# Rows of x by products of 64x32 tiles in the last three batches, with a new planner rule and a new table

## The chip, the core and the metric

The kernel runs on one core of a Trainium2 chip. The core has a matrix engine (TensorE, "PE" in the profile, its weight loads "PEld"), three engines for element-wise work (VectorE "DVE", ScalarE "ACT", GpSimd "POOL") and queues that start DMAs (here nearly all from "SP"). TensorE reads SBUF and writes PSUM; VectorE and ScalarE copy from PSUM to SBUF. The metric is the device time of one execution in microseconds. The median of three runs before the change is 265.24 us (264.93 to 265.75).

## What is computed

The reference is an attention of the Nystrom kind over eight batches, eight heads, 576 tokens of 64 elements, followed by a layer with a norm, two weight matrices and a residual:

```
q_lm, k_lm = means of q, k over 32 segments of 18 tokens
A = softmax(q k_lm'), Bm = softmax(q_lm k_lm'), C = softmax(q_lm k')
Z = Bm' / (norms);  six times: Z = 2 Z - Z Bm Z
x = A Z C v                       per head, then laid out as (batch, 576, 512)
out = x + relu(norm(x) * g @ w1) @ w2      w1 512 x 2048, w2 2048 x 512
```

The change concerns how `x` is formed in the last three batches. For a batch, `x` is 576 rows of 512 columns. Each head gives 64 of the columns: the head's 32 columns of A (one for each landmark) times a 32 x 64 matrix, Z C v. `x` is needed for the statistics of the norm and for the residual; the first layer does not read it, because the kernel multiplies A by a product that it has already folded with w1.

## The kernel before, in words

**Tiles.** The rows of `x` of all batches lie in blocks of 128 (`x_blk`), 36 in all. A batch has 4.5 blocks: odd batches begin with half a block and even batches end with one. Four heads are handled as a unit `u` of 128 partitions, 32 landmarks each, so a batch has two units. For each unit `ea[u]` holds the scores of q (landmarks on partitions, tokens along the free axis), and `zcbd[u]` the matrix Z C v of its four heads, written block by block on the diagonal of a 128 x 256 tile; the rest of that tile is zero.

**Rows.** `rows_of` (line 808) forms one block at a time: two products of 128 x 128 weights (`ea`) and 256 columns (`zcbd`), one for each unit, into one bank of PSUM; then one copy of 512 columns to `x_blk`, on ScalarE or VectorE, whichever the planner expects to be done sooner (`sooner`). It is the last part of `attention2`, which forms the attention of one or two batches. `measure` then takes a block's statistics on VectorE, and `deviations` turns them into the factors of the norm that `finish_block` needs.

**First layer.** `First.two_products_of_heads` (line 1341) forms two of the four `m16` tiles of a batch: sixteen products of 64x32 tiles and 512 columns, eight of which run side by side, into two banks and one double bank, `psm`; four copies of 512 columns follow. It is called twice a batch. `chunk` then makes one of 16 row tiles of the hidden layer: four products of 288 columns into a double bank `psh`, and one copy with a relu to `hT`. All double banks are drawn from a pool of two (`ps2`, tag `p2`); the other four banks are handed out by `banks`.

**Second layer.** It multiplies `hT` by w2. From batch 4 on it uses seven products of halves in place of eight (`seven_products`), for which VectorE mixes parts of `hT` and GpSimd mixes parts of w2 ahead. The last 64 columns of an even batch's `hT` are copied by GpSimd into the next batch's (`keep_tail`).

**Order.** The kernel writes out one order of instructions for each engine. Five streams (attentions, totals, first layers, first rows, second layers) are generators; before each step a stream says when it could go, and `run` takes the first that can. The times come from a planner, class `Clock`: `note` books every instruction with an estimated duration (`took`) on its engine. Small work (loads, casts, turns, statistics, mixes) is put in between by `help_out`. The table `AFTER` holds exceptions found by search: an entry (k, n): (j, m) keeps the n-th step of kind k back until m steps of kind j are done. In `took`, an operation of VectorE of 1024 elements is given a longer time when GpSimd is busy; and after a centring of w1 the planner moves the time at which GpSimd is free.

**Buffers of zcbd.** There are four. A batch that is handled alone takes two of them by its parity, a pair of batches takes all four.

All VectorE, ScalarE and GpSimd instructions that the planner records have the helper's line 302 in the profile, and the matmuls line 308, so that groups are told apart by the names of tiles: `bank<-zcbd,ea` are the rows, `bank<-w,zt` and `psm<-w,zt` the products of heads, `psh<-ea,m` the chunks, `bank<-w,hT` and `bank<-w2mix` the second layer.

Of the kernel before, what the change touches and what calls it, by code (L numbers as in the profile page):

```python
# [10 lines left out]
FP32 = mybir.dt.float32  # L11
# [5 lines left out]
P = 128  # L17
# [3 lines left out]
def kernel(  # L21
# [63 lines left out]
    class Clock:  # L85
# [5 lines left out]
        def __init__(self):  # L91
            self.free = dict.fromkeys(("PE", "DVE", "Activation", "Pool", "SP"), 0.0)
            self.wrote, self.used, self.begun = {}, {}, {}
            self.small, self.lanes, self.wire = False, {}, 0.0
            self.cells, self.count, self.mark, self.fetched, self.ahead = [], 0, 95, 0.0, 0.0
            self.loads, self.pool = [], []
            self.free['PE'], self.issued = 1500.0, 0
# [33 lines left out]
        def took(self, i, e, n, m):  # L131
# [25 lines left out]
        def note(self, i):  # L157
# [70 lines left out]
            else:  # L228
                start = max(self.free[e], ready)
                self.ready = start  # L230
# [4 lines left out]
                if e == 'DVE' and count[0] == 1024 and writes[0] in parted_w1:  # L235
                    self.free['Pool'] = max(self.free['Pool'], start) + 430
# [573 lines left out]

    def rows_of(bs, ea, zcbd):
# [288 lines left out]
    def attention2(bs, c):  # L1100
# [113 lines left out]
        cv, z0 = cv_[0], 2 * (bs[0] % 2) if W == 2 else 0  # L1214
        yield lambda: clock.both(clock.at(st, cv), asm.next("zt"))
# [38 lines left out]
        yield from rows_of(bs, ea, zcbd_buf[z0:z0 + W])  # L1254
# [9 lines left out]
    def block_done(j):  # L1264
        unmeasured.append(j)

    def measure():
        j = unmeasured.pop(0)
        b, u = group_of(j)
        if u == 0:  # L1270
# [4 lines left out]
        blocks_done[b] = u + 1  # L1275
# [55 lines left out]
    class First:  # L1331
# [60 lines left out]
    def first_layer(b):  # L1392
# [5 lines left out]
        if two:  # L1398
            yield lambda: max(banks.next(2), ps2.next("p2"), mprod.next("m16", 2), clock.at(l1.zt))
            l1.two_products_of_heads(0)  # L1400
        else:
            yield lambda: max(banks.next(2), mprod.next("m16"), clock.at(l1.zt))
            l1.product_of_heads(0)
        for m in range(MCH):
            yield lambda: max(ps2.next("p2"), clock.at(l1.m16[m // 4], *l1.ea))
            l1.chunk(m)
            chunks[b] = m + 1
# [5 lines left out]
            if two and m == 4:  # L1413
                yield lambda: max(banks.next(2), ps2.next("p2"), mprod.next("m16", 2))
                l1.two_products_of_heads(2)
# [5 lines left out]
    chunks = {}  # L1421
# [242 lines left out]
    def help_out(hurry=False):  # L1664
# [226 lines left out]
```

## Time and profile before

| | |
|---|---|
| median of the runs | 265.24 us |
| the profiled execution, its own time | 265.93 us |
| its span, first to last instruction | 264.2 us |
| TensorE busy | 253.6 us, 3351 matmuls |
| VectorE busy | 209.4 us |
| ScalarE busy | 173.2 us |
| GpSimd busy | 136.0 us |
| rows of x, products | 80 of 128x256 |
| rows of x, copies of a whole block | 22 on ScalarE (596 ns), 10 on VectorE (688 ns) |

The profile is of one execution. Its page lists busy times by engine, a chain of the work that ended last, and groups of equal instructions with their mean duration and the idle time of the engine ahead of them. Matmuls are pipelined: their durations overlap, so what one occupies is read from the starts in the timeline. The timeline gives the start, the duration and, in brackets, how long the engine had stood idle and what ended that.

### The profile page before, as it was taken

What the parts mean: (1) busy time and instruction counts of PE and PEld (TensorE: products, weight loads), DVE (VectorE), ACT (ScalarE), POOL (GpSimd) and SP (SyncE); (2) the same over time, 40 slices, a digit from 0 to 9 for tenths busy, and PEclk for the clock granted to TensorE, in tenths of its full rate; (3) what the DMA queues carried; (4) which work ended last, traced back from release to release, by engine and by line L of the source; (5) the groups of instructions that cost most, each with busy time, mean ns of one, the idle gap of its engine ahead of it and who ended that gap; (6) DMA issues with size and microseconds to landing.
All of it is one profiled execution on the core that took longest, in us unless ns stands there. A gap on an engine that the chain in (4) does not pass through costs nothing.

```text
span 264.2 us, 8212 instructions
## 1 busy us (share of the span) xinstructions
PE 253.6 (96%) x3351; PEld 167.7 (63%) x3351; DVE 209.4 (79%) x466; ACT 173.2 (66%) x333; POOL 136.0 (51%) x162
## 2 busy tenths in 40 slices
PE   7899989999999999999999999999999999999994
PEld 6645754546456574546655466577877875788883
DVE  2677865999979987999998974999696868976762
ACT  2588886548686987588788687667666755873000
POOL 5288779999861889797799956600000005000000
PEclk9999999999999999999999999999999999999999
DMA  7999999999867896866951010110060006100605
GB/s 249 381 394 369 383 389 372 357 265 325 286 176 211 264 365 172 262 182 169 398 147 45 21 47 19 42 40 4 0 159 4 2 21 144 38 0 2 159 16 185
DMA packets 24125, 46.67 MB, mean 177 GB/s; under 512 B 2964, under 2 KB 3224, under 8 KB 24088
## 3 DMA queue, kind: packets, MB, share of 16 engines
q1 hardware_dynamic: 23608, 45.50, 54.0%
q10 hardware_dynamic: 480, 0.66, 0.8%
q8 instruction: 26, 0.43, 0.7%
q14 instruction: 11, 0.09, 0.1%
HBM read 36.70 MB, written 9.44 MB: 175 GB/s over the span
## 4 chain that ended last, share of the span: by engine, by line
PE 75%; DVE 11%; DMA 8%; ACT 2%; POOL 2%; issue 1%; SPq 0%; DVEq 0%
PE bank L308 49%; PE psh L308 20%; DMA stg<-in_k_dram 4%; DMA wstg<-in_moe_w_ch_dram 4%; DVE m L302 2%; DVE w L302 2%; PE pscv L308 2%; PE psd L308 2%; DVE xblk L302 1%; DVE six L302 1%; DVE part L302 1%; POOL w L302 1%; PE psea L308 1%; ACT lns L302 1%; DVE xT L302 1%
## 5 line engine op out<-in xcount | busy, mean ns | idle before, releaser
L308 PE MATMUL bank<-w,hT 128*128 128x512 f16 (+3 forms) x528 | 110.2, 335 | 0.0
L302 ACT ACTIVATE hT<-psh 128x576 f16<-128x576 f32 x119 | 74.3, 653 | 20.9 <-PE psh L308 19.2
L308 PEld LDWEIGHTS <-hT 128*128 128x128 f16 x656 | 60.8, 98 | 30.5 <-issue 5.7
L308 PE MATMUL psh<-ea,m 128*128 128x288 f16 x512 | 78.7, 286 | 0.1
L308 PEld LDWEIGHTS <-m 128*128 128x128 f16 x512 | 49.1, 98 | 19.1 <-issue 1.9
L302 DVE SCALAR_TENSOR_TENSOR xblk<-bank,rstd,xblk 128x256 f32<-128x256 f32 (+2 forms) x77 | 38.9, 540 | 12.6 <-PE bank L308 12.3
L302 POOL TENSOR_TENSOR ea<-ea,lns 128x576 f16<-128x576 f16 x14 | 17.9, 1286 | 52.0 <-ACT lns L302 51.6
L302 POOL CAST nat<-stg 128x1152 f16<-128x1152 f32 x23 | 26.9, 1186 | 12.9 <-DVE xT L302 7.1
L302 DVE BATCH_NORM_STATS2 six<-xblk 128x6 f32<-128x512 f32 x36 | 24.2, 673 | 1.7 <-ACT xblk L302 1.6
L302 POOL CAST natv<-stg 128x1152 f16<-128x1152 f32 (+1 forms) x17 | 19.3, 1163 | 11.0 <-DMA stg<-in_v_dram 7.8
L302 ACT COPY xblk<-bank 128x512 f32<-128x512 f32 (+1 forms) x29 | 16.6, 592 | 8.6 <-PE bank L308 8.4
L302 DVE STREAM_TRANSPOSE xT<-nat 128x576 uint32<-128x576 uint32 x28 | 21.3, 761 | 0.3 <-POOL nat L302 0.3
L302 DVE SCALAR_TENSOR_TENSOR st<-st,bank 128x128 f16<-128x128 f16 (+3 forms) x36 | 13.2, 366 | 9.2 <-PE bank L308 9.0
L308 PE MATMUL bank<-w2mix 128*128 128x256 f16 x128 | 17.9, 273 | 0.0
L308 PE MATMUL bank<-w2mix,hT 128*128 128x256 f16 x128 | 16.4, 272 | 0.0
L302 ACT ACTIVATE lns<-psd 128x576 f32<-128x576 f32 x16 | 10.3, 646 | 6.5 <-PE psd L308 6.3
L302 DVE TENSOR_REDUCE part<-xT 128x32 f16<-128x576 f16 x20 | 14.3, 740 | 0.1
L308 PE MATMUL bank<-zcbd,ea 128*128 128x256 f16 x80 | 14.3, 273 | 0.0
L308 PEld LDWEIGHTS <-st 32*32 32x32 f16 (+1 forms) x380 | 7.0, 90 | 11.4 <-DVE st L302 6.9
L308 PEld LDWEIGHTS <-w2mix 128*128 128x128 f16 x128 | 12.4, 98 | 2.5 <-issue 0.6
L302 POOL TENSOR_TENSOR asum<-asum 128x256 f32<-128x256 f32 (+1 forms) x20 | 12.8, 641 | 1.6
L302 ACT CAST m<-bank 128x512 f16<-128x512 f32 x16 | 9.2, 587 | 6.5 <-PE bank L308 6.3
(130 smaller groups left out, 372.2 us busy)
## 6 DMA issues: line engine op xcount, KB each, us to landing
stg<-in_q_dram SPq DMA_DIRECT2D x16, 576.0 KB, 6.4
stg<-in_k_dram SPq DMA_DIRECT2D x16, 576.0 KB, 6.1
out_dram<-xblk SPq DMA_DIRECT2D x66, 128.0 KB, 2.4
wstg<-in_moe_w_ch_dram SPq DMA_DIRECT2D x16, 512.0 KB, 7.6
stg<-in_v_dram SPq DMA_DIRECT2D x5, 576.0 KB, 8.5
stg<-in_v_dram SPq DMA_DIRECT2D x40, 72.0 KB, 3.0
stg<-in_v_dram SPq DMA_DIRECT2D x6, 288.0 KB, 5.1
stg<-in_v_dram SPq DMA_DIRECT2D x12, 144.0 KB, 4.0
```

The costliest lines, as they stand in the source:

```text
L302: return lambda *args, **kw: keep(getattr(self.engine, op)(*args, **kw))
L308: keep(nc.tensor.matmul(o, l, r, start=start, stop=stop, tile_position=(rb, cb), skip_group_check=(skip or cb != 0)))
```

## The change

It has three parts.

1. In batches 5 to 7 (`LATER = 5`) the rows of `x` are no longer formed by `attention2`. `rows_later` only notes which blocks there are and keeps `ea` and `zcbd`. `two_rows` forms two whole blocks at once, right behind `two_products_of_heads` (at both of its calls, `PAIRS = (0, 4)`), from 32 products of 64x32 tiles and 128 columns into one double bank `psr`; four copies of 256 elements for the two blocks, strided on the side of `x`, follow behind the copies of the products of heads. The contraction is over 64 partitions, that is two heads, and not 128. The half block of a batch is still formed by whole products (`part_of_rows`), behind chunk 8 of an even and chunk 6 of an odd batch. Four whole blocks in each of three batches make six groups.
2. In the planner, a centring of w1 no longer moves GpSimd's free time; it books an interval (`locks`), and a GpSimd operation that would begin inside of it begins at its end. An operation of 1024 elements on VectorE right behind such an interval is given 1600 ns in place of 1000 when GpSimd is busy for over 1000 ns more.
3. The table `AFTER` is new, with 67 entries (72 before), most of them different. The choice of `zcbd` buffers is new too: a batch alone takes the first two except batch 1, and an attention waits until rows that are still to be formed no longer need the buffers. `measure` counts blocks in place of taking the last one's number.

```diff
+    def crossed(x, hp):
+        n = 256 + 64 * (1 - 2 * hp)
+        v = x[:, 64 * hp:64 * hp + DM - 128]
+        return bass.AP(v.tensor, v.offset, [list(v.ap[0]), [n, 2], [2 * D, 2], [1, D]])
+
+    def two_rows(b):
+        ea, zcbd = row_zc[b]
+        mine = [row_blocks[b].pop(0) for _ in range(2)]
+        t = ps2.tile([P, 2, 512], FP32, name="psr", tag="p2")
+        to = t[:].rearrange("p h (i u c) -> p h i u c", i=2, u=U)
+        for i in range(2):
+            for u in range(U):
+                for c in range(4):
+                    for hp in range(2):
+                        MM(to[ds(32 * c, 32), hp, i, u, :],
+                           ea[u][ds(64 * hp, 64), ds(mine[i][1] + 32 * c, 32)],
+                           zcbd[u][ds(64 * hp, 64), :, :]
+                           .rearrange("p (r e) d -> p r e d", e=2)[:, :, hp ^ u, :],
+                           rb=64 * hp, cb=32 * c, skip=True)
+
+        def copies():
+            copy = sooner(1024, clock.at(t))
+            for i, (j, _) in enumerate(mine):
+                for hp in range(2):
+                    copy(crossed(x_of(j), hp), to[:, hp, i, :, :].rearrange("p u (r d) -> p u r d", r=2))
+                block_done(j)
+        return copies
...
             one = self.products(f, [banks.take([P, 512]), t[:, 0, :]])
             two = self.products(f + 1, [banks.take([P, 512]), t[:, 1, :]])
+            copies = two_rows(self.b) if 2 * f in PAIRS and self.b >= LATER else lambda: None
             self.copies(f, one)
             self.copies(f + 1, two)
+            copies()
...
-        cv, z0 = cv_[0], 2 * (bs[0] % 2) if W == 2 else 0
-        yield lambda: clock.both(clock.at(st, cv), asm.next("zt"))
+        cv, z0 = cv_[0], 2 * (bs == (1,))
+        mine_z = {name_of(t) for t in zcbd_buf[z0:z0 + W]}
+        yield lambda: (NEVER if any(name_of(t) in mine_z for _, z in row_zc.values() for t in z)
+                       else clock.both(clock.at(st, cv), asm.next("zt")))
...
-        yield from rows_of(bs, ea, zcbd_buf[z0:z0 + W])
+        yield from (rows_later if bs[0] >= LATER else rows_of)(bs, ea, zcbd_buf[z0:z0 + W])
...
             l1.chunk(m)
+            if m == PART[b % 2] and b in row_part:
+                part_of_rows(b)
...
                 last = max([b for a, b in self.pool if a <= self.ready < b] + [0.0])
-                queued = 1000 if self.free["Pool"] > self.ready else 690
+                next_ = self.locks and self.ready - self.locks[-1][1] < 150
+                queued = (690 if self.free["Pool"] <= self.ready else
+                          1600 if next_ and self.free["Pool"] > self.ready + 1000 else 1000)
...
+                if e == "Pool":
+                    for a, z in self.locks:
+                        if a <= start < z:
+                            start = z
...
                 if e == 'DVE' and count[0] == 1024 and writes[0] in parted_w1:
-                    self.free['Pool'] = max(self.free['Pool'], start) + 430
+                    self.locks = self.locks[-4:] + [(start, done)]
...
-    chunks = {}
+    chunks, PART, PAIRS, ONES = {}, (8, 6), (0,4), ()
+    LATER = 5
```

In the instructions: 24 products of 128x256 go and 192 of 64x32 tiles with 128 columns come, so that TensorE has 3519 matmuls in place of 3351. Twelve copies of whole blocks of rows become 24 copies of 256 elements, 16 on VectorE and 8 on ScalarE in the new order.

More of the change, by code (lines that the diff above doesn't have):

```diff
@@ L809, in iterate, with rows_later @@
         return stn
+    row_blocks, row_part, row_zc = {}, {}, {}
+    def rows_later(bs, ea, zcbd):
+        for i, b in enumerate(bs):
+            row_blocks[b] = []
+            row_zc[b] = ea[U * i:U * i + U], zcbd[U * i:U * i + U]
+            t0 = 0
+            while t0 < S:
+                j, pb = divmod(b * S + t0, P)
+                n = min(P - pb, S - t0)
+                if n == P:
+                    row_blocks[b].append((j, t0))
+                else:
+                    row_part[b] = j, pb, n, *((t0 + n - P, P - n) if pb == 0 else (0, 0))
+                t0 += n
+        for _ in range(5 * len(bs)):
+            yield lambda: 0.0
@@ new lines, in one_row, with part_ready, part_of_rows @@
+    def one_row(b):
+        ea, zcbd = row_zc[b]
+        j, at = row_blocks[b].pop(0)
+        xb = x_of(j)
+        psy = banks.take([P, 512])
+        for u in range(U):
+            MM(psy[:, ts(u, 4 * D)], ea[u][:, ds(at, P)], zcbd[u][:].rearrange("p h d -> p (h d)"))
+        sooner(512, clock.at(psy))(xb[:], psy)
+        block_done(j)
+    def part_ready(b):
+        return max(banks.next(2), 0.0 if row_part[b][0] in x_blk else xpool.next("xblk"))
+    def part_of_rows(b):
+        ea, zcbd = row_zc[b]
+        j, pb, n, at, side = row_part.pop(b)
+        xb = x_of(j)
+        psy = banks.take([P, 512])
+        for u in range(U):
+            MM(psy[:, ts(u, 4 * D)], ea[u][:, ds(at, P)], zcbd[u][:].rearrange("p h d -> p (h d)"))
+        sooner(512, clock.at(psy))(xb[ds(pb, n), :], psy[ds(side, n), :])
+        if pb + n == P:
+            block_done(j)
@@ L1404, in first_layer @@
         for m in range(MCH):
-            yield lambda: max(ps2.next("p2"), clock.at(l1.m16[m // 4], *l1.ea))
+            yield lambda: max(ps2.next("p2"), clock.at(l1.m16[m // 4], *l1.ea),
+                              part_ready(b) if m == PART[b % 2] and b in row_part else 0.0,
+                              max(banks.next(2), xpool.next("xblk")) if m in ONES and b >= LATER else 0.0)
             l1.chunk(m)
+            if m == PART[b % 2] and b in row_part:
+                part_of_rows(b)
+            if m in ONES and b >= LATER:
+                one_row(b)
+            if b in row_zc and not row_blocks[b] and b not in row_part:
+                row_zc.pop(b)
             chunks[b] = m + 1
```

14 lines of the change are left out of this document (10 added, 4 removed), and 33 rows, old and new, of the table AFTER.

## The prediction

> **What bounds the kernel now.** I read the page first (busy times, the chain of work that ended last), then the groups by form for the price of one instruction, then the timeline at the few places where TensorE stands still. The page says what kind of kernel this is:
>
> ```profile
> span 264.2 us, 8212 instructions
> PE 253.6 (96%) x3351; PEld 167.7 (63%) x3351; DVE 209.4 (79%) x466; ACT 173.2 (66%) x333; POOL 136.0 (51%) x162
> ...
> PE 75%; DVE 11%; DMA 8%; ACT 2%; POOL 2%; issue 1%; SPq 0%; DVEq 0%
> ```
>
> TensorE is busy 96% and holds 75% of the chain; from 72 us to the end the chain is almost TensorE alone. So a change pays by the matmul time that it removes, and by the places where TensorE waits. The granted clock is 1.00 in every stage, so columns turn into time at one rate. The prices, from the groups by form (last columns: busy us, mean ns of one, idle before):
>
> ```profile
> L308 PE MATMUL bank<-zcbd,ea 128*128 128x256 f16 x80 | 14.3, 273 | 0.0
> L308 PE MATMUL bank<-w,zt 64*32 64x512 f16 x144 | 10.9, 383 | 1.2 <-DVE xblk L302 0.9 <-ACT zt L302 0.3
> L302 ACT ACTIVATE ec<-psec 128x256 f16<-128x256 f32 x28 | 10.8, 474 | 0.9 <-PE psec L308 0.7
> L302 ACT COPY xblk<-bank 128x512 f32<-128x512 f32 x22 | 12.6, 596 | 3.9 <-PE bank L308 3.8
> L302 DVE COPY xblk<-bank 128x512 f32<-128x512 f32 x10 | 6.9, 688 | 1.6 <-PE bank L308 1.6
> L302 DVE TENSOR_TENSOR zcbd<-pszc,heads 128x256 f16<-128x256 f32 x14 | 5.0, 414 | 0.0
> L302 ACT CAST zt<-pszt 128x256 f16<-128x256 f32 x1 | 0.4, 353 | 0.0
> ```
>
> The mean of a pipelined matmul is latency; what it occupies is read from starts in the timeline (start us, us, engine, form):
>
> ```profile
> 74.00 0.72 PE L308 MATMUL pscv<-natv,ecT 64*64 64x130 f16 x36
> 74.66 0.42 PE L308 MATMUL psd<-ea,bones 128*128 128x288 f16 x2
> ...
> 82.55 0.38 PE L308 MATMUL bank<-zcbd,ea 128*128 128x256 f16 x2
> 82.77 0.38 PE L308 MATMUL bank<-w,hT 128*128 128x512 f16 x1
> ```
>
> Two whole products of 256 columns occupy 0.22 us, 0.11 each. Thirty-six products of 64x64 tiles and 130 columns, four at a time, are nine rounds: of the 0.66 us from 74.00 to 74.66 about 0.10 is the change of tile shape, which leaves 0.062 a round. By columns at the whole product's rate (0.11 for 256) a round would be 0.055.
>
> TensorE's largest wait after the start, in the timeline around the rows of batch 5:
>
> ```profile
> 169.21 2.15 DVE L302 TENSOR_TENSOR w2mix<-hT 128x1024 f16<-128x1024 f16 x2
> 169.78 1.04 POOL L302 COPY hT<-hT 128x1024 f16<-128x1024 f16 x1 [1.47 <-PE bank L308]
> ...
> 171.28 0.74 DVE L302 SCALAR_TENSOR_TENSOR xblk<-bank,rstd,xblk 128x512 f32<-128x512 f32 x1
> ...
> 172.07 0.37 PE L308 MATMUL bank<-w,zt 64*32 64x512 f16 x1 [0.93 <-DVE xblk L302]
> ```
>
> Two mixes on VectorE (0.68 each elsewhere) take 2.15 beside a copy on GpSimd, the update of x behind them starts late, its bank comes free at 172.02, and the second round of products of heads starts at 172.07 where 170.95 was possible: 1.1 us lost. Two smaller ones:
>
> ```profile
> 45.31 0.23 PE L308 MATMUL pszt<-st,cv 32*32 32x32 f16 x16
> 45.85 0.22 PE L308 MATMUL pszc<-cv,st 32*32 32x64 f16 x8 [0.31 <-ACT lns L302]
> ...
> 70.66 0.19 PE L308 MATMUL bank<-st,bones 128*128 128x64 f16 x1
> 71.40 0.29 PE L308 MATMUL bank<-st 128*128 128x128 f16 x2 [0.55 <-DVE st L302]
> ```
>
> About 0.4 us at 45 and, with 0.13 ahead of 70.66, 0.84 at 70.
>
> **The change part by part.** *The products.* Twelve blocks of rows (batches 5 to 7) lose 24 whole products: 24 x 0.110 = 2.63 us. They get 192 products of 64x32 tiles and 128 columns, eight tiles at a time, so 24 rounds in six groups of four. By columns a round is 0.055; at the spread of the 64x64 rows (0.062 for 130 columns) it is 0.061; the first round of that row, whose weights are loaded in the open, took about 0.08. The groups stand straight behind products of heads of the same 64x32 shape, and the order of the changed kernel has as many changes of tile shape as before (58), so none is added. I take 0.060, since weights for the first round can load during the 0.21 us of the round ahead: 24 x 0.060 = 1.44, **gain 1.2**; bounds 1.3 (0.055) and 0.7 (0.08). *The page's price:* "TensorE: Matmul & The Clock Gate" of the Trainium skill, Back-to-back issue gap, gives some 81 ns between matmuls of 128 columns in a stream of loads and matmuls; taken as the price of a round, the gain would be 0.7. No run here has that stream, and the 64x64 rows (0.062 a round) speak for less.
>
> *The copies.* Twelve copies of 512 become 24 of 256 strided elements, 16 on VectorE and 8 on ScalarE in the new order. VectorE: 16 x 0.42 = 6.7; ScalarE: 8 x 0.35 to 0.47 = 2.8 to 3.8. With the other copies shifted between them (whole-block copies 10 to 3 and 22 to 17, half blocks 1 to 4 and 7 to 4, first-layer outputs 9 to 6 and 119 to 122) VectorE gains about 1.7 us of work (6.7 - 4.8 + 2.1 - 2.3) and ScalarE stays within 1 us. Both have room as a total, so this costs only where TensorE waits for a copy.
>
> *The buffer.* A group's output takes the second of the two double-bank buffers that the chunks of the first layer rotate through. The second chunk behind a group therefore waits for its four copies, and the first for the copies of the products of heads. Hand-over costs 0.17 from TensorE (mean 286 for a 288-column matmul of 0.12) and 0.05 back (172.02 to 172.07). From the order: behind the first group of batch 7, TensorE has sixteen 256-column products and a change of shape (1.85 us) before the first chunk, and about 3.0 before the second. ScalarE alone carries four copies of products of heads (4 in 2.16 at 168.44, or 4 x 0.60), then four row copies (0.29 apart as the exps at 36.05, six in 1.74, or 0.47 each): the first chunk's buffer is free 1.9 to 2.2 after the group, the second's 3.1 to 4.0. I take 0.6 us of waiting here, 0.2 behind the first group of batch 5 (same four copies on ScalarE, rows on VectorE), 0.1 each behind the two of batch 6 (0.69 + 4 x 0.42 + 0.22 - 0.27 = 2.3 against 2.2 of cover), none behind the other two: **cost 1.0**, bounds 0 and 3.6 (below).
>
> *The wait at 172.* The rows of batch 5 no longer take banks before these products, and in the new order the last reader of either bank has 3 us or more of TensorE work between its input and the reuse. **Gain 1.1**; 0 if VectorE is as late again.
>
> *The new table.* It moves nearly everything after 32 us: loads, casts, turns, mixes. The SP queue issues the same DMAs with some stores and loads exchanged; DMA has room from 135 us on (share about 0.2). I looked at each wait above again. At 45 a pair of second-layer products now stands between, **gain 0.4** (0 to 0.5). At 70 VectorE has one centring of w and one statistics ahead of the softmax, not two centrings (0.98 mean each, 1.90 for the pair at 67.45): **gain 0.4** of 0.84 (0 to 0.84). At 35 the old wait of about 1.4 stays, in another form: a chunk now stands straight behind the scores and must wait for three exps. In batches 5 and 6 five chunks return to their buffer after 0.82 us of TensorE work, where the output's 0.653 and the 0.22 to 0.24 of hand-over need 0.89: **cost 0.35** (0 to 0.7).
>
> **The sum.** -1.2 + 1.0 - 1.1 - 0.4 - 0.4 + 0.35 = -1.75 us against the profiled execution: 265.93 to 264.2. That execution lies 0.69 above the median of 265.24, so the median goes to **263.5**.
>
> **The rivals.** *Evacuation turns into the bound (slower).* TensorE saves 0.2 us a group but every group now waits. This is a rule of "TensorEngine Tiling (Array Packing)" of the Trainium skill, Performance Considerations: tiles speed up TensorE and not the emptying of PSUM, which may become the bottleneck. In rows: if VectorE comes to the four groups that it copies about 0.6 later (at 171.28 it was over 1 us late beside GpSimd) and ScalarE's row copies cost 0.47 with its queue, the waits are 4 x 0.6 + 1.0 + 0.2 = 3.6 instead of 1.0: 263.5 + 2.6 = 266.1. It ends slower than before once the six groups wait over 2.75 in all, 0.46 each. For it: 79% busy VectorE. Against it: 1.85 to 4 us of cover in the order.
> *The waits only move.* The mixes and GpSimd's copies are the same instructions, and 2.15 for 1.36 of work shows what they do to a queue. If the new order has as much waiting as the old one where I see none, the gains of 1.1, 0.4 and 0.4 go: 263.5 + 1.9 = 265.4, or 264.5 if half of it comes true.
> *The tiles do not overlap.* If each round shows its weight load (89 ns for a 64x32 load, mean of the groups) before its 0.055, 24 x 0.145 = 3.5: 0.85 lost instead of 1.2 won, 263.5 + 2.05 = 265.5. The 64x64 rows speak against it.
>
> **How the numbers follow.** Forecast 0.52 (own range 262.4 to 264.4); evacuation 0.15; waits move 0.20, of which 0.05 stay under 264.4; no overlap 0.07; better than forecast (all waits gone, no new ones: 261.7) 0.06. A difference under 0.3% (0.8 us) is about what a measurement can't tell from none. Faster: 0.52 + 0.06 + 0.05 = 0.63. Within: 0.13 + 0.07 = 0.20. Slower: 0.15 + 0.02 = 0.17. The range reaches from 262.3 to 265.8: below it most of the 0.06, above it most of the evacuation.
>
> **What would show it.** Groups of four rounds that take 0.22 to 0.27 us; the two rounds of products of heads of batch 5 side by side; chunk tiles behind the groups with waits for copies of the row tile of 0.2 to 0.6 in batch 7; no wait of 0.5 us for a softmax in batch 2. Wrong would be: rounds above 0.08; waits for row copies of over 0.4 behind every group; a wait of over 1 us anywhere after 72 us.

## The result, and the profile after

The changed kernel takes 263.31 us in the median of eight runs (263.06 to 264.70). Beside them on the same chip the kernel before took 265.38 (eight runs, 264.93 to 265.75). The ratio is 0.9929 with a 95% interval of 0.9911 to 0.9947: 0.7% faster, 2.07 us.

The profiled execution of the changed kernel has an own time of 264.70 us, 1.4 above its median, where that of before lay 0.7 above. So its span is only 1.2 us shorter. The page:

```profile
span 263.0 us, 8556 instructions
PE 252.0 (96%) x3519; PEld 167.8 (64%) x3519; DVE 209.7 (80%) x475; ACT 171.5 (65%) x335; POOL 137.3 (52%) x163
...
PE 75%; DVE 10%; DMA 8%; ACT 3%; issue 1%; POOL 1%; SPq 0%; ACTq 0%; DVEq 0%
```

Nothing about the bound has changed: TensorE is busy 96% and holds 75% of the chain. It does 1.6 us less. The new groups, by form (busy us, mean ns of one, idle before):

```profile
L315 PE MATMUL bank<-zcbd,ea 128*128 128x256 f16 x56 | 9.9, 273 | 0.0
L315 PE MATMUL psr<-zcbd,ea 64*32 64x128 f16 x192 | 3.0, 217 | 0.0
L309 DVE COPY xblk<-psr 128x256 f32<-128x256 f32 x16 | 5.6, 414 | 0.0
L309 ACT COPY xblk<-psr 128x256 f32<-128x256 f32 x8 | 2.5, 432 | 0.0
L315 PE MATMUL psh<-ea,m 128*128 128x288 f16 x512 | 78.5, 286 | 1.0 <-ACT ec L309 0.9
```

Of the whole products of rows 56 are left. The copies cost what was predicted (0.42 and 0.35 to 0.47). The chunks (`psh`) stand idle for 1.0 us in all, and 0.9 of that is for exps at 35 us, not for row copies.

The place of the largest wait before, the products of heads of batch 5, in the timeline of after (start us, us, engine, form, idle before):

```profile
168.36 1.29 DVE L309 TENSOR_TENSOR w2mix<-w2mix,hT 128x1024 f16<-128x1024 f16 x2
169.32 1.23 POOL L309 COPY hT<-hT 128x1024 f16<-128x1024 f16 x1 [3.96 <-PE bank L315]
169.56 0.74 DVE L309 SCALAR_TENSOR_TENSOR xblk<-bank,rstd,xblk 128x512 f32<-128x512 f32 x1
...
169.67 0.39 PE L315 MATMUL bank<-w,zt 64*32 64x512 f16 x1
...
169.89 0.38 PE L315 MATMUL bank<-w,zt 64*32 64x512 f16 x1
...
170.11 0.48 PE L315 MATMUL psr<-zcbd,ea 64*32 64x128 f16 x32
...
170.53 1.92 PE L315 MATMUL bank<-w,hT 128*128 128x256 f16 x16
...
171.62 1.40 DVE L309 COPY xblk<-psr 128x256 f32<-128x256 f32 x4
```

The two rounds stand side by side (169.67, 169.89), where before 1.1 us lay between them. The two mixes ahead of the update of x take 1.29 us here, where before 2.15 stood, with GpSimd's copy of `hT` starting when they are nearly done; the update begins at 169.56 and not at 171.28. The second round does not even wait for it: the update ends at 170.30, the round starts at 169.89. By the semaphores in the trace (the signals by which one engine waits for another), its product into a bank waits for ScalarE, whose last signal came at 168.15; before, it waited for VectorE's at 172.03. The four rounds of rows begin at 170.11. From the first product of heads to the next whole product is 0.86 us (169.67 to 170.53). Products of heads without rows take 0.56 (46.41 to 46.97), so the rows cost 0.30 here; in batch 6 the same reading gives 0.88 (191.38 to 192.26), 0.32.

The two smaller places:

```profile
45.61 0.24 PE L315 MATMUL pszt<-st,cv 32*32 32x32 f16 x16
...
45.72 0.22 PE L315 MATMUL pszc<-cv,st 32*32 32x64 f16 x8
...
70.04 0.21 DVE L309 TENSOR_REDUCE rsum<-bank 128x2 f32<-128x64 f32 x1
...
70.36 1.15 POOL L309 TENSOR_TENSOR asum<-nat 128x512 f32<-128x512 f16 x1
...
70.77 0.19 PE L315 MATMUL bank<-st,bones 128*128 128x64 f16 x1 [0.60 <-DVE st L309]
71.03 0.76 DVE L309 TENSOR_TENSOR st<-bmT,mask 128x256 f16<-128x256 f16 x1
...
71.85 0.28 PE L315 MATMUL bank<-st 128*128 128x128 f16 x2 [0.89 <-DVE st L309]
```

The wait at 45 is gone. The one at 70 is not: TensorE stands still twice, 0.77 and 1.06 us counted from when the work ahead has run through, where before it was 0.13 and 0.72.

So the time is there, but not where I had put it. Theory A for the experiments: tiles and the place of the rows bring the gain. Its rival B: the new table does, and the tiles add nothing. Two smaller questions go with them: why a round costs 0.075 to 0.08 and not 0.06, and why the softmax of batch 2 got later.

### The profile page after: what moved, and what is told of

It is laid out like the page before. It is cut to its first block, busy times and chain, and to the rows that moved or that the text cites. A ratio compares the mean times of both kernels' runs of the same rounds, so it can differ in the third digit from the quotient of the medians.

```text
span 263.0 us, 8556 instructions
## 1 busy us (share of the span) xinstructions
PE 252.0 (96%) x3519; PEld 167.8 (64%) x3519; DVE 209.7 (80%) x475; ACT 171.5 (65%) x335; POOL 137.3 (52%) x163
## 4 chain that ended last, share of the span: by engine, by line
PE 75%; DVE 10%; DMA 8%; ACT 3%; issue 1%; POOL 1%; SPq 0%; ACTq 0%; DVEq 0%
PE bank L315 49%; PE psh L315 19%; DMA wstg<-in_moe_w_ch_dram 6%; DVE m L309 2%; DMA stg<-in_k_dram 2%; DVE w L309 2%; PE pscv L315 2%; PE psd L315 2%; ACT xblk L309 1%; DVE six L309 1%; PE psea L315 1%; DVE xblk L309 1%; DVE part L309 1%; ACT hT L309 1%; PE psec L315 1%
## 5 line engine op out<-in xcount | busy, mean ns | idle before, releaser
L309 ACT ACTIVATE hT<-psh 128x576 f16<-128x576 f32 x122 | 75.9, 653 | 22.5 <-PE psh L315 21.1
L309 POOL CAST nat<-stg 128x1152 f16<-128x1152 f32 x24 | 28.9, 1223 | 9.8 <-DMA stg<-in_v_dram 4.7
L315 PE MATMUL bank<-w2mix 128*128 128x256 f16 x128 | 17.3, 273 | 0.0
L309 ACT COPY xblk<-bank 128x512 f32<-128x512 f32 (+1 forms) x21 | 12.4, 594 | 5.9 <-PE bank L315 5.8
L309 ACT ACTIVATE ec<-psec 128x256 f16<-128x256 f32 (+1 forms) x42 | 11.9, 424 | 2.3 <-PE psec L315 2.0
```

What stands on the lines that cost most here:

```text
L309: return lambda *args, **kw: keep(getattr(self.engine, op)(*args, **kw))
L315: keep(nc.tensor.matmul(o, l, r, start=start, stop=stop, tile_position=(rb, cb), skip_group_check=(skip or cb != 0)))
```

## The experiments

**The changed kernel once more.** No edit.

> The changed kernel once more, unaltered, beside the kernel before on one chip. Both theories (the gain sits in the rows and the wait at 172; the gain sits in the new table) expect the same of it: 263.3 us, ratio to before 0.993. What it tells is how steady the places are: the wait of 1.34 us before bank<-nat,pairs at 25.9 (0.57 in the profile of before, where the instructions up to there are the same) should be back near 0.6 if it is an accident of one execution, and the two waits around the softmax of batch 2 (0.77 and 1.06 us, together 1.8 against 0.84 before) should stay at 1.8 if they belong to the new order, or fall to about 0.4 as predicted if they too are an accident.

263.56 us, ratio 0.9927 (0.9909 to 0.9945). The wait at 26 us was 0.78 in this execution. In the runs below, with the same program up to there, it was between none and 1.07: its length changes from one execution to the next, and 0.8 of the high time of the first profile is such an accident. The two waits of batch 2 stayed here, 0.78 and 1.05. But the next three runs have the same instructions up to the rows of batch 5, and there they are 0.89 and 0.71, 0.57 and 0.71, 0.48 and 0.72. So 0.4 to 0.8 us over the 0.84 of before belong to the order, and the rest to the execution; the last section shows what makes the second wait 1.05 or 0.71.

**Whole products in the same places.** The rows of the six groups by 24 whole products again. The planner still books the tiles, so that every engine keeps the order of the changed kernel; the copies now take adjacent columns (412 ns on VectorE and 432 on ScalarE; 414 and 432 with tiles).

```diff
-        for i in range(2):
-            for u in range(U):
-                for c in range(4):
-                    for hp in range(2):
-                        MM(to[ds(32 * c, 32), hp, i, u, :], ...)
+        for i in range(2):
+            for u in range(U):
+                MM(t[:, i, ds(256 * u, 256)], ea[u][:, ds(mine[i][1], P)],
+                   zcbd[u][:].rearrange("p h d -> p (h d)"), skip=True)
```

> The rows of the six groups are made by whole products again (four of 128x128 with 256 columns a group, copied out by four copies of 256), in the places and in the order of the changed kernel on every engine; only the tiles are undone. Theory A (the tiles pay what the trace of the change shows, 0.300 to 0.326 us a group, 1.88 in all, against 24 x 0.110 = 2.63 for whole products): 0.75 us slower than the changed kernel, so about 264.1, plus up to 0.1 us a group if the whole products make TensorE change its tile shape once more (about 0.10 at a change by the rows of 64x64 tiles at 74.0), which gives 264.1 to 264.7. The predicted price of 0.060 a round: 1.2 us slower, 264.5 (to 265.1). Theory B (the new table brings the gain, the tiles nothing): 263.3, no difference from the changed kernel.

264.18 us, ratio 0.995 (0.9934 to 0.9966): 0.62 above the run beside it. The two intervals overlap a little, but the traces agree with the size: a group of whole products takes 0.45 (168.92 to 169.37 in its timeline), of tiles 0.30 to 0.32, and from the last products of heads of batch 4 (at 145 to 146 us) to the last matmul the profiled execution takes 0.74 more. So the tiles are worth 0.6 to 0.75 us, a third of the gain, and not the 1.2 that was predicted. The softmax of batch 2 in this execution:

```profile
70.05 0.42 DVE L310 TENSOR_TENSOR st<-bmT,mask 128x256 f16<-128x256 f16 x1
...
70.53 0.29 PE L318 MATMUL bank<-st 128*128 128x128 f16 x2 [0.55 <-DVE st L310]
```

Here the multiplication by the mask takes 0.42 us and not 0.76: GpSimd's `asum` begins behind it, at 70.18.

**Half of the rows between the two rounds.** Sixteen of a group's 32 tile products stand between the two rounds of products of heads. The planner books them behind both rounds as before, so that nothing else moves.

```diff
-            one = self.products(f, [banks.take([P, 512]), t[:, 0, :]])
-            two = self.products(f + 1, [banks.take([P, 512]), t[:, 1, :]])
...
+                half, copies = two_rows(self.b)
...
+                one = self.products(f, [banks.take([P, 512]), t[:, 0, :]])
...
+                half(0)
...
+                two = self.products(f + 1, [banks.take([P, 512]), t[:, 1, :]])
...
+                half(1)
```

> The first half of a group's row products (two rounds of tiles) stands between the two rounds of products of heads, the second half behind them; nothing else is moved on any engine. Theory A (the loads of the tiles are issued ahead only as far as they gained on the longer products of heads; in the trace of the change the first three rounds start 55 to 56 ns apart, and in the fourth each of the eight products comes 8.4 ns behind the one before): every half has a long round ahead of it, so all four rounds take some 56 ns, 0.225 us a group instead of 0.300 to 0.326: 0.45 to 0.6 us faster than the changed kernel, about 262.8. Theory B (78 ns is simply what a round of eight such products costs): no difference, 263.3.

263.15 us, ratio 0.9916 (0.9896 to 0.9935), 0.41 below the changed kernel beside it. The two intervals overlap, so the timeline has to decide. The same place as above:

```profile
169.27 0.39 PE L317 MATMUL bank<-w,zt 64*32 64x512 f16 x1
...
169.50 0.29 PE L317 MATMUL psr<-zcbd,ea 64*32 64x128 f16 x16
169.61 0.38 PE L317 MATMUL bank<-w,zt 64*32 64x512 f16 x1
...
169.82 0.29 PE L317 MATMUL psr<-zcbd,ea 64*32 64x128 f16 x16
170.05 0.72 PE L317 MATMUL bank<-w,hT 128*128 128x256 f16 x5
```

From 169.27 to 170.05 is 0.78 in place of 0.86, and all six groups measure the same: rows cost 0.22 a group, 0.055 a round. In the changed kernel the single starts are 0, 55 and 111 ns for the first three rounds, and then the fourth comes one product at a time: 186, 195, 203, 211, 220, 228, 236, 270. Inside of the first three rounds neighbours are 2 to 5 ns apart. So 0.055 is what a round costs, and what was added in the changed kernel is a shortage in the fourth round in a row. Theory A holds: the length of the row of tile products makes it. The load records of the changed kernel say more, the same in all six groups. Each tile product has its own weight load. In the first round a load starts 214 ns ahead of its product, in the second and third 54 ns. In the fourth only the first load is early (73 ns); the other seven start 4 to 5 ns ahead of their products (the last one or two 30), one between every two of them. So the fourth round goes at the pace of its loads. With halves the same late loads turn up in the third round, but they fall under the second round of products of heads, and are still 82 to 140 ns ahead of their products. Why the loads stop being early after 25 is not in the traces.

**Copies done twice.**

```diff
                     copy(crossed(x_of(j), hp), to[:, hp, i, :, :]...)
+                    copy(crossed(x_of(j), hp), to[:, hp, i, :, :]...)
```

> Each of the 24 copies of rows out of the row tile is done twice over, one straight behind the other on the same engine; the order is otherwise that of the changed kernel. Theory A (the copies are covered: the chunks behind a group waited 0.09 to 0.22 us at four groups and not at the other two): VectorE gets 16 x 0.4 = 6.4 us and ScalarE 8 x 0.3 = 2.4 us more; per group 1.2 to 1.7 us more before the buffer is free, of which the cover that the order leaves (the 0.4 to 1.5 us by which the copies were early) takes a part: 0 to 0.8 us a group, 1 to 4 us in all, 264.5 to 267.5. Theory B (emptying the row tile already sets the pace, the rival of the prediction): every group pays the full 1.2 to 1.7 us, 7 to 10 us in all, 270 to 273.

269.15 us, ratio 1.0137 (1.0117 to 1.0157): 5.6 us more, between the two theories. The groups by form show where:

```profile
L318 PE MATMUL psh<-ea,m 128*128 128x288 f16 x512 | 78.7, 286 | 5.6 <-ACT hT L312 1.5 <-DVE xblk L312 1.5 <-ACT xblk L312 1.4
```

The chunks wait 4.6 us more than in the changed kernel. Counted from the end of a group to the fourth chunk behind it, the six groups pay 1.2, 0, 1.0, 1.6, 1.5 and 0.25 us. The copies had grown by about 1.8 us a group on VectorE (1.40 to 3.23 at the first group) and 1.6 on ScalarE, which copies the second group of batch 5 and the first of batch 7. How much cover was left (time by which the copies are done before TensorE wants the buffer) can be read in the changed kernel itself: the second chunk behind a group, which takes the row tile's buffer, starts 0.08, 1.93, 0.12, 0.25, 0.13 and 0.94 us after the last copy has ended, some 0.05 of which is the hand-over. So three of the six groups have under 0.1 us of cover. For ScalarE's two groups this fits the growth: with 1.9 of cover nothing is paid, with 0.1 it is 1.5. At three of VectorE's four less is paid than the growth beyond the cover, because this run does not only double copies. The first group:

```profile
170.02 3.23 DVE L312 COPY xblk<-psr 128x256 f32<-128x256 f32 x8
170.69 0.65 PE L318 MATMUL psh<-ea,m 128*128 128x288 f16 x4
...
171.38 0.65 ACT L312 ACTIVATE hT<-psh 128x576 f16<-128x576 f32 x1 [0.78 <-PE psh L318]
172.08 0.65 PE L318 MATMUL psh<-ea,m 128*128 128x288 f16 x4 [0.41 <-ACT hT L312]
...
173.31 0.65 PE L318 MATMUL psh<-ea,m 128*128 128x288 f16 x4 [0.47 <-DVE xblk L312]
```

The second chunk waits for the first one's output here, and only the third for the copies: the chunks have taken the two buffers in another order than in the changed kernel. The emptying of the row tile is covered, but just: the rival that it becomes the bound was nearer than the trace lets one think at first sight.

**Two centrings of w behind the softmax of batch 2.** An edit on VectorE's queue alone; the planner books the two centrings where they were.

```diff
     def center_w1(f, c):
...
-        dve.tensor_tensor(out=o, in0=o, in1=less(f)[:, None, :].broadcast_to([P, 2, 512]),
-                          op=ALU.add)
+        by = less(f)[:, None, :].broadcast_to([P, 2, 512])
+        if f == 1:
...
+            put_off.append(lambda: tc.keep_in_program_order(
+                nc.vector.tensor_tensor(out=o, in0=o, in1=by, op=ALU.add)))
+        else:
+            dve.tensor_tensor(out=o, in0=o, in1=by, op=ALU.add)
...
     def whole_iterate(p1, st, it):
...
+        if it in (1, 2) and put_off:
+            put_off.pop(0)()
```

> The changed kernel with two centrings of w (the ones that VectorE did at 64 and 68.4 us, ahead of the softmax of batch 2) put off on VectorE until behind the first and the second step of the iteration of batch 2 (about 74 and 76 us, where VectorE stood still 0.4 to 0.5 us at a time); nothing is moved on any other engine. Theory A (VectorE, busy 98% from 48 to 76 us, sets the time of the softmax, so what the new order gained ahead of 70 us and the products that it no longer has between scores and softmax turn up as the two waits of 0.6 to 0.9 and 0.7 to 1.06 us): about 2 us of VectorE's work go from in front of rsum; the first wait goes, the second falls to the hand-over that before shows too (0.55 to 0.72) or less: 0.9 to 1.4 us faster than the changed kernel, about 262.3. Theory B (the softmax waits for ScalarE, whose exp stands behind lnv and a cast, or for the hand-overs themselves): the waits stay within 0.2 us, 263.4.

262.83 us, ratio 0.9906 (0.9891 to 0.9921). That is 0.73 below the changed kernel's 263.56, which was measured on another chip; by the ratios to the kernel before (265.37 and 265.56 beside them) it is 0.56. The timeline of batch 2:

```profile
67.98 0.22 DVE L310 TENSOR_REDUCE rsum<-bank 128x2 f32<-128x64 f32 x1 [0.86 <-ACT bank L310]
...
68.97 0.43 DVE L310 TENSOR_TENSOR st<-bmT,mask 128x256 f16<-128x256 f16 x1
69.30 0.19 PE L316 MATMUL bank<-st,bones 128*128 128x64 f16 x1
...
69.46 0.28 PE L316 MATMUL bank<-st 128*128 128x128 f16 x2
...
75.23 1.35 DVE L1418 TENSOR_TENSOR w<-w,less 128x1024 f16<-128x1024 f16 x1
...
77.05 0.31 PE L316 MATMUL bank<-st 128*128 128x160 f16 x2 [0.39 <-DVE st L310]
```

Now VectorE waits for the exp (0.86) and not the other way round; both waits of TensorE are gone but for 0.13. So VectorE set the time of the softmax, as theory A says. A part was given back: the second centring took 1.35 us beside GpSimd, the step behind it came late, and TensorE lost 0.55 us at 77. That is enough to make the gain 0.6 to 0.7 and not 0.9 to 1.4.

**Both edits.**

> Both edits at once: the halves of the row products between the two rounds of products of heads, and the two centrings of w behind the softmax. If the two causes are separate (rounds from 169 us on, VectorE before 72 us), the gains add: 0.4 from the first (0.41 between the medians of that run and the changed kernel beside it) and 0.9 to 1.4 from the second, so 261.6 to 262.2. If time gained early is given back to a later limit (one execution with the halves showed a wait of 1.1 us at 116 to 118 for lns from ScalarE behind ea from GpSimd), the sum is smaller, 262.4 to 263.1.

262.29 us, ratio 0.9889 (0.9873 to 0.9905), and 262.53, 0.9881 (0.9858 to 0.9904), when run again below. It lies just above the 261.6 to 262.2 of added gains, since the centrings had brought less than expected. It is 0.54 under the run with the centrings alone, where the halves had brought 0.41 alone, and in the traces the halves take 0.4 less from batch 4 to the end in both pairs: the two causes are separate and their gains add. The wait of 1.1 us at 116 that one execution with the halves had shown is not in it. This version beats both kernels.

**Rows alone.** Tiles and places of the change, old rule, old table.

```diff
-                next_ = self.locks and self.ready - self.locks[-1][1] < 150
-                queued = (690 if ... 1600 if next_ and ... else 1000)
+                queued = 1000 if self.free["Pool"] > self.ready else 690
...
-                    self.locks = self.locks[-4:] + [(start, done)]
+                    self.free['Pool'] = max(self.free['Pool'], start) + 430
...
-        (0, 17): (4, 31), (0, 23): (4, 75), ...
+        (0, 17): (4, 31), (0, 23): (4, 77), ...
```

> The rows by tiles behind the products of heads, with the planner's old rule for VectorE beside GpSimd and the old table. Theory A (tiles and their place bring the gain): the groups cost 0.30 to 0.33 us each as in the changed kernel (0.75 less than whole products), the rows of batch 5 take no banks ahead of its products of heads (1.1 less), and the waits at 45 and 70 stay as before: 1.85 under before, about 263.6, ratio 0.993. Theory B (the table brings it, and the old table fits the new instructions badly): 265 or more, not faster than before, with new waits of over 0.5 us where the old entries now fall on other instructions.

267.11 us, ratio 1.0068 (1.0055 to 1.0081): slower than before. Theory A fell in this form. The timeline at the products of heads of batch 5:

```profile
168.35 0.38 PE L309 MATMUL bank<-w,zt 64*32 64x512 f16 x1
...
168.57 0.51 PE L309 MATMUL psr<-zcbd,ea 64*32 64x128 f16 x32
...
169.60 1.40 DVE L303 COPY xblk<-psr 128x256 f32<-128x256 f32 x4
...
171.53 1.28 DVE L303 TENSOR_TENSOR w2mix<-w2mix,hT 128x1024 f16<-128x1024 f16 x2
...
172.73 1.28 DVE L303 TENSOR_TENSOR hT<-hT 128x1024 f16<-128x1024 f16 x2
173.93 0.86 DVE L303 SCALAR_TENSOR_TENSOR xblk<-bank,rstd,xblk 128x256 f32<-128x256 f32 x2
...
174.85 1.14 PE L309 MATMUL bank<-w2mix 128*128 128x256 f16 x9 [0.97 <-DVE xblk L303]
```

The wait between the rounds is gone here too. But the four row copies (1.40 us) now stand on VectorE ahead of five mixes and the update of x, and a product of `w2mix` waits 1.14 us for that update's bank. The same comes back at 249 (1.13). From 164 us to the end this kernel takes 1.2 us more than before, though not more work: summing what lies between matmuls beyond their columns, the waits there are 3.65 us against 1.69. The rest, 0.7 us, is in its favour, and that is what the rows save.

**The table alone.** The rows of batches 5 to 7 by whole products as before (`LATER = 99`), new rule and new table.

> The new rule and the new table with the rows of batches 5 to 7 by whole products as before, in places of their own. Theory A (tiles and place): 0.75 for the whole products and the wait at 172 (1.1) come back, unless the new order gives VectorE's update of x more time there: 264.2 to 265.4. Theory B (the new order by itself brings the gain): 263.5, no slower than the changed kernel, and no wait of over 0.5 us at the products of heads of batch 5.

266.72 us, ratio 1.0049 (1.0032 to 1.0066): slower than before, too, so B falls as well; it is also 1.3 us above the range of theory A. Here, also, the rounds of products of heads of batch 5 follow each other (170.25 and 170.48 in its timeline). From 160 us to the end it takes 3.06 us more than the changed kernel: 2.44 of that are waits (3.23 against 0.79), scattered in pieces of 0.25 to 0.4 us between 178 and 249; the rest, 0.6, is about what the whole products cost more.

**Rule and table apart.** Rows by tiles with the new rule and the old table; then with the old rule and the new table.

> Rows by tiles and the planner's new rule for VectorE beside GpSimd, with the old table. Theory A (the table has to be written for the order that the rows make; the rule does little): as the run with rows alone (267.1), 266 to 268, with waits of 0.5 us or more at products of w2mix behind the groups. Theory B (the rule, which puts GpSimd's work out of the way of VectorE's centrings, mends what the rows do to VectorE's queue): 265 or less, without the two waits of 1.1 us of the run with rows alone.

> Rows by tiles and the new table, with the planner's old rule. Theory A (the table carries it, the rule does little): within 1 us of the changed kernel, 263 to 264.5. Theory B (table and rule belong together, since the entries of the table count instructions in an order that the rule shapes): 265 or more, with new waits of 0.5 us or more from 40 us on, where the rule first acts (the first centrings of w beside GpSimd).

268.86 us, ratio 1.0137 (1.0104 to 1.0169), and 274.82, 1.0352 (1.032 to 1.0384). The first is 0.9 us above the range of theory A, with the two waits at `w2mix` as it said (1.14 and 1.13 us); for the second theory B holds, by far. The table counts steps in an order that rule and rows make, so under another order its entries hold back other steps than those they were found for; that this is what made the waits was not followed entry by entry. With the old rule, waits of 0.4 to 1.6 us came at 114, 131 to 138, 179 and 232 to 235 us. So what was measured of one part alone is that part in an order that nobody has adjusted, not its share in the gain.

**The put-off centrings one step earlier**, in the version with both edits, which ran again beside it.

```diff
     def whole_gram(psse_, st):
...
+        if put_off:
+            put_off.pop(0)()
         return cinv, csum
...
-        if it in (1, 2) and put_off:
+        if it == 1 and put_off:
```

> The version with both edits once more, beside the next one on one chip: 262.3 us, ratio 0.989. The wait of 0.55 us before the third step of the iteration of batch 2 (77.05 in the run with the centrings put off, behind a centring of 1.35 us on VectorE beside GpSimd's ea) should be there again.

> Both edits, but the two put-off centrings one step earlier: the first straight behind the scaling of the Gram matrix, the second behind the first step of the iteration. Theory A (a put-off centring costs only where it stands between a step's matmul and its update on VectorE; behind the Gram matrix TensorE has the products of pscv, 1.6 us of work, before it wants the first step's update, and the second centring takes 0.69 at that place, not 1.35): the wait of 0.55 us goes, 261.8. Theory B (VectorE has no time left before 77 us, wherever the centrings stand): a wait of 0.4 us or more turns up at another step, 262.3.

262.53 us again for both edits, with the wait of 0.55 us at the same step. The earlier place gave 263.35, ratio 0.9913 (0.9891 to 0.9935): worse than either theory said. A wait turned up at another step, as in theory B, and there is a reason that is in neither:

```profile
68.90 1.15 POOL L310 TENSOR_TENSOR asum<-nat 128x512 f32<-128x512 f16 x1
...
69.14 1.19 DVE L310 TENSOR_TENSOR st<-bmT,mask 128x256 f16<-128x256 f16 x1
...
70.39 0.29 PE L318 MATMUL bank<-st 128*128 128x128 f16 x2 [0.73 <-DVE st L310]
...
71.91 1.61 POOL L310 CAST nat<-stg 128x1152 f16<-128x1152 f32 x1
72.43 1.63 DVE L310 TENSOR_TENSOR w<-w,less 128x1024 f16<-128x1024 f16 x1
...
75.17 0.31 PE L318 MATMUL bank<-st 128*128 128x160 f16 x2 [0.62 <-DVE st L310]
```

The multiplication by the mask, the same instruction as at 68.97 above (0.43), took 1.19 us because GpSimd had begun a sum 0.24 us ahead of it. The centring that now follows the put-off one took 1.63 (0.68 in the changed kernel) beside a cast, and TensorE waited 0.78 us for the update of the first step. The first of these stands ahead of the moved centrings, so it is chance in this execution; the second is of the edit.

## Why the total was right and most parts were not

The sum of the prediction against what the two profiled executions show (us, minus is a gain; the waits are what lies between matmuls beyond their columns and changes of tile shape):

| step of the prediction | predicted | measured |
|---|---|---|
| rows by tiles | -1.2 | -0.75 |
| waits for the row copies behind the six groups | +1.0 | 0 |
| waits there for outputs of chunks (`hT`) | 0 | +0.5 |
| wait at 172 | -1.1 | -1.1 |
| wait at 45 | -0.4 | -0.3 |
| softmax of batch 2 (wait at 70) | -0.4 | +1.0 (+0.4 to +0.8 in three other executions) |
| five chunks returning to their buffer, batches 5 and 6 | +0.35 | under 0.1 |
| waits not spoken of: 31 to 37 (-0.5), 54 to 58 (-0.5), 75 (-0.3), 203 to 217 (-0.2), groups of small tiles that now stand together (-0.3), new ones at 61, 88 and 157 (+0.5) | 0 | -1.3 |
| wait at 26, by execution | 0 | +0.8 |
| sum | -1.75 | -1.15 of -1.2; the rest in small pieces |

Without the accident at 26 us the two executions would differ by 2.0 us; the medians differ by 2.07. The forecast of 263.5 missed 263.31 by 0.2 because errors of both signs cancelled: that it came so near is luck.

*The products.* Right in kind: the tiles overlap, no change of tile shape was added, and the rival without overlap is out. Mis-sized: 24 rounds took 1.88 and not 1.44. The step that failed is "I take 0.060, since weights for the first round can load during the 0.21 us of the round ahead". That was true of the first three rounds (55 ns, loads 54 to 214 ns ahead) and not of the fourth. The upper bound of 0.08 was the one that came nearest, and groups of 0.22 to 0.27 us, named as the sign of the forecast, were 0.30 to 0.32. "TensorE: Matmul & The Clock Gate" of the Trainium skill, Back-to-back issue gap, with its 81 ns for 128 columns, comes near the mean of 78 ns as I had applied it. It does not describe what happens: with half as many tile products in a row the same rounds take 55.

*The copies and the buffer.* The durations were right, and the waits did not come: in the changed kernel no chunk waits for a copy of rows. What waits there is (0.14 and 0.08 us behind the first group of batch 6, 0.09 behind its second, 0.22 behind the second of batch 7) is for ScalarE's output of an earlier chunk in the same buffer. Behind the first group of batch 7, where 0.6 was put, the copies were done 2.9 us after the group and not 3.1 to 4.0, against a cover of 3.05: the estimate was near the edge, on the wrong side. For chunks that return to their buffer the prediction had 0.35, but at five others in batches 5 and 6, where there was next to nothing.

*The wait at 172.* Gone, but the reason was only half of it. I said that the rows of batch 5 no longer take banks there. The table alone, with the rows at whole products and taking banks, removes it as well, and so do the rows alone. By the semaphores it is the last reader of the bank that changed. Before, the second round waited for VectorE. In the changed kernel and with the table alone its product into a bank waits for ScalarE, whose last signal lies 1.7 and 1.3 us back (168.15 for 169.89, 169.22 for 170.48); with the rows alone it carries no wait. So the other half of the reason, that the last reader is done long before, is what holds.

*The wait at 70.* The step that failed most: "VectorE has one centring of w and one statistics ahead of the softmax, not two centrings". I looked at what stands directly ahead. Busy time by stretches, of before and then of after (columns: stretch, its length, PE, PEld, DVE, ACT, POOL busy us, granted clock, DMA share, GB/s):

```profile
48.00:72.00 24.00, 23.36 (x229) 13.24 (x226) 23.59 (x44) 15.77 (x32) 22.25 (x24) 1.00 0.95 307
```

```profile
48.00:72.00 24.00, 22.40 (x197) 12.95 (x195) 23.59 (x43) 15.81 (x32) 22.89 (x25) 1.00 1.00 321
```

From 48 to 72 us VectorE is busy 23.59 of 24 us in both kernels. What counts is all that it has to do by then. The run with whole products shows it best, since its wait at 26 us (0.56) is that of before (0.57). `rsum` begins there at 69.07, 0.87 us earlier than the 69.94 of before. TensorE, without the wait at 45 and with nine products of 512 columns between scores and softmax where there were twelve, is through with them at 68.90 and not at 70.53, 1.63 earlier; it only came to wait there sooner. Its own busy time from 48 to 72 fell by 1.0 in the changed kernel. Putting two centrings behind the softmax removed both waits. So some 0.8 of the 1.6 us went back into this wait: in front of an engine that has no time left, a wait that goes comes back, in part, at the next thing that this engine delivers.

*The waits only move* was given 0.20, and did happen at this one place. Elsewhere the new order has fewer of them.

*That the tiles make the kernel faster* is true only together with the table: rows alone are 0.7% slower than before, the table alone 0.5%. In each of the orders a group of rows by tiles costs 0.30 to 0.33 us (but for one group in the run with the old rule), so the rows' own saving of 0.6 to 0.75 us is there; what waits the order makes decides whether it is kept.

## What to carry to other kernels

Before a wait is booked as a gain, look at whether the engine that ends it, or the next wait behind it, has a pause at all in that stretch; if it has none, sum its work up to there instead of reading what stands just ahead. Put small tile products in short rows between longer ones: 16 in a row behind a round of 512 columns cost 0.055 us a round of eight, 32 in a row 0.078. And where an order was tuned for a set of instructions, a part taken alone measures the order that it spoils; compare waits and work separately, or hold the order fixed, as the runs with whole products and with halves did. And look at a wait in several executions before it is put down to the order: here two waits of the same program were 1.2 us long together in one execution and 1.8 in another.

## What the runs showed of the hardware that was not expected

*VectorE beside GpSimd.* The multiplication `st<-bmT,mask` took 0.42 to 0.43 us alone, 0.76 in the changed kernel and 1.19 in the last run. In the second and third cases GpSimd's `asum<-nat` (1.15 us) had begun first, at 70.36 and 68.90, and ended at 71.51 and 70.05. The multiplication ended at 71.79 and 70.33, both times 0.28 us later. So it is not slowed in proportion; it stands still until the other is done. The Trainium skill says so on "SBUF — State Buffer", Who interferes with whom: a VectorE instruction with two inputs in SBUF and a GpSimd instruction that reads SBUF share a port, and the one that comes later is blocked for the whole of the other. These two cases agree with it. It also makes the cost of an order depend on which of two engines comes first by 0.2 us.

The other executions bear this out. The multiplication ended the same 0.28 us behind GpSimd in the second execution of the changed kernel, with the table alone and with the new rule and the old table (0.76 to 0.77 us long), and behind a shorter operation of GpSimd where both edits ran again (0.59). Where it came first, by 0.05 us before the change, it took 0.42, and GpSimd's sum 1.39 in place of 1.15. This is also what makes the second wait of batch 2 long or short: it is 1.05 to 1.06 us in the four executions in which the multiplication took 0.76 to 0.77, and 0.71 to 0.72 in the six in which it took 0.42 (the runs with the centrings put off aside).

*The granted clock.* In the run with the old rule and the new table TensorE waited 0.86 and 0.90 us within 2.5 us behind the first group of batch 7, after 0.41 just ahead of that group. Busy time and clock by stretches of that run (columns as above):

```profile
231.00:233.00 2.00, 1.62 (x75) 0.76 (x75) 2.00 (x5) 1.16 (x3) 0.00 (x0) 1.00 0.35 82
233.00:234.90 1.90, 0.65 (x4) 0.39 (x4) 1.90 (x6) 1.16 (x3) 0.00 (x0) 1.00 0.04 9
235.00:238.30 3.30, 3.19 (x15) 2.10 (x15) 0.98 (x4) 1.36 (x3) 0.00 (x0) 0.55 0.00 0
```

The clock fell to 0.55 in the mean of the 3.3 us that follow, in which TensorE was busy again: some 1.5 us more, on top of the waits. The waits of 0.77 and 1.06 us within 1.9 us at 70 in the changed kernel did not lower it. The profile of the new rule with the old table has a stretch at 0.50 too, from 17.0 to 20.4 us, behind a wait of 1.06 us. What tells these cases apart was not tried.
